# Two of the first-layer weight transfers put on ScalarE's queue, the last weight piece moved forward on SyncE's, and half a dummy matmul ahead of layer 1

## Chip, cores, metric

One core of one Trainium2 chip. The metric is device time in microseconds (us) of one execution. A run counts as slow when it lies over 1.5% above the fastest of the same kernel. Some kernels lose a stretch of full TensorE clock in some runs, and each run's mean granted clock (1.0, or less) tells which. Where a kernel has both kinds of run, its full-clock runs are compared with full-clock runs.

## The reference

```python
B, S, D, F = 1, 2048, 448, 1792            # x, w1 [D,F], b1, w2 [F,D], b2, all bf16
def reference(x, w1, b1, w2, b2):
    h = jnp.einsum("bsd,df->bsf", x, w1) + b1
    h = gelu_tanh(h)
    return jnp.einsum("bsf,fd->bsd", h, w2) + b2
```

## The kernel before

The 2048 rows go through in four chunks of 512. For the first chunk x is loaded plainly and turned by TensorE; the other chunks come by transposing transfers. D = 448 is three blocks of 128 rows of w1 and a remainder of 64. The matmuls use half the array's rows each (64 of 128) and run in pairs. F is 14 tiles of 128 columns. w1's three full blocks arrive in three pieces: tiles 0 to 3 (384 KB), 4 to 7 (384 KB), 8 to 13 (576 KB). The 64 remainder rows arrive in two: tiles 0 to 3 (64 KB) and 4 to 13 (160 KB), and VectorE copies some of each to the other half of the partitions.

```python
        W1CUTS = (0, 4, 8, 14)
        def load_w1(i):
            c0, c1 = W1CUTS[i] * P, W1CUTS[i + 1] * P
            pr.dma("sync", lambda e: e.dma_start(
                w1_sb[:, :, c0:c1], w1[0:D3, c0:c1].rearrange("(k p) f -> p k f", p=P)), ("w1", i))
        RCUTS = (0, 4, 14)
        def load_w1r(i): ...                      # the remainder rows, same form
        # ... (cut)
        pr.dma("sync", lambda e: e.dma_start(xn[:, :, :], x0v), "x")
        load_w1(0)
        load_w1r(0)
        load_w1(1)
        load_w1r(1)
        load_w1(2)
        load_w2(0, 7)
        load_w2(7, 14)
        # ... (cut): b2, then the transposing loads of x
        pr.dma("scalar", ... b1n ..., after=["b1z"])
        pr.op("scalar", lambda e: e.activation(junk[:, :], one, ACT.Gelu_apprx_tanh))   # brings the table load
        # ... (cut)
        warm(NWARM)          # 7 dummy matmuls of 512 columns
        warm(1, HC)          # and one of 256, while x comes
        turn_all()           # 12 + 2 transposes of x, copied out by VectorE and ScalarE
        turn_b1()
        # ... (cut)
        for h in (0, HC):    # layer 1, chunk 0: pairs of F tiles L[0], L[1], ...
            L[0].a(h, h + HC)
            L[1].a(h, h + HC)
        L[0].b()             # ends with the remainder rows
        L[2].a()             # first use of w1's second piece
        L[1].b()
        for j in range(3, NPAIR):
            L[j].a()         # L[4].a: first use of the last piece
            L[j - 1].b()     # L[2].b: first use of the second remainder rows
```

## Time and profile before

| | before |
|---|---|
| time, median of 3 runs | 94.44 us (94.21 to 94.9) |
| span of the profiled run | 93.3 us |
| TensorE busy | 90.0 us, 96% |
| TensorE idle from the first layer-1 matmul to the last | none |
| first piece of w1 issued, landed | 1.18, 6.0 us |
| second piece of w1 issued, landed, used | 2.25, 7.85, 7.99 us |

In the chain of work that ended last each line is a start, a duration and what ran or was waited for. In the timeline the bracket at the end of a line holds how long the engine stood still just before and what released it. SPq and ACTq are the DMA issues of SyncE and ScalarE; a merged line "x2" is two instructions in a row. The two 384 KB pieces of w1 have the same name (w_sb), and are told apart by their issue time.

### The profile page before, as it was taken

Reading aid. Unit: us, or ns where it says so; the run is one execution under the profiler, and the core shown is the slowest. Engines: PE = TensorE matmul, PEld = TensorE weight load, DVE = VectorE, ACT = ScalarE, POOL = GpSimd, SP = SyncE. Lnnn points to the kernel's source line nnn. Section 1 sums busy time; section 2 is a strip of 40 time slices with the busy share of each in tenths; the row PEclk is TensorE's granted clock in tenths of the full one; section 3 lists DMA queues with packets and bytes.
Section 4 is the critical chain, followed back from the end, with each engine's and each line's share of the span. In section 5 each row is a group of like instructions: output and inputs, shape, how many; then the busy total and the mean of one; then the engine's idle time right before and its main releaser. Section 6 shows DMA issues by size and latency. Waiting matters only on the chain.

```text
span 93.3 us, 2058 instructions
## 1 busy us (share of the span) xinstructions
PE 90.0 (96%) x931; PEld 46.6 (50%) x931; DVE 13.4 (14%) x33; ACT 38.5 (41%) x63; POOL 1.1 (1%) x7
## 2 busy tenths in 40 slices
PE   6989999999999999999999999999999999999990
PEld 2475444555554444555554444555554444475890
DVE  0174001100333000000334000000234000000421
ACT  3373787800003787900002887900001878910001
POOL 4000000000000000000000000000000000000000
PEclk9999999999999999999999999999999999999999
DMA  2999999645657000000033000000022000000022
GB/s 48 323 270 303 378 342 137 124 102 113 63 97 212 0 0 0 7 0 0 0 102 101 0 0 4 0 7 0 0 98 98 0 7 0 0 0 7 19 79 98
DMA packets 12340, 7.32 MB, mean 78 GB/s; under 512 B 6956, under 2 KB 12140, under 8 KB 12332
## 3 DMA queue, kind: packets, MB, share of 16 engines
q1 hardware_dynamic: 12304, 7.20, 31.5%
q8 instruction: 7, 0.11, 0.5%
q14 instruction: 1, 0.01, 0.0%
q10 hardware_dynamic: 28, 0.00, 0.0%
HBM read 3.79 MB, written 1.84 MB: 60 GB/s over the span
## 4 chain that ended last, share of the span: by engine, by line
PE 96%; ACT 1%; DVE 0%; issue 0%
PE u L215 91%; PE u L190 4%; PE u L337 1%; ACT xT L344 1%; DVE out_sb L324 0%
## 5 line engine op out<-in xcount | busy, mean ns | idle before, releaser
L267 ACT ACTIVATE g<-u,b_f 128x512 bf16<-128x512 f32 x56 | 35.0, 685 | 40.1 <-PE u L215 40.1
L215 PE MATMUL u<-w_sb,g 64*128 64x448 bf16 (+1 forms) x504 | 43.2, 328 | 0.0
L215 PE MATMUL u<-xT,w_sb 64*128 64x512 bf16 (+1 forms) x348 | 40.9, 369 | 0.3 <-ACT xT L344 0.3
L215 PEld LDWEIGHTS u<-w_sb,g 64*128 64x128 bf16 x504 | 24.5, 94 | 18.4
L215 PEld LDWEIGHTS u<-xT,w_sb 64*128 64x128 bf16 x348 | 16.9, 94 | 19.4 <-DMA w_sb<-in_w_dram 0.6
L310 DVE TENSOR_TENSOR out_sb<-u,b_bc 128x448 bf16<-128x448 f32 x14 | 8.1, 620 | 60.8 <-PE u L215 60.8
L215 PE MATMUL u<-xT,w1r 64*128 64x512 bf16 x56 | 10.6, 376 | 0.0
L215 PEld LDWEIGHTS u<-xT,w1r 64*128 64x128 bf16 x56 | 2.8, 94 | 3.4
L327 ACT CAST out_sb<-u 128x224 bf16<-128x224 f32 x1 | 0.3, 345 | 9.2 <-PE u L215 9.2
L190 PE MATMUL u<-const-bfloat16-1.0 128*128 128x512 bf16 (+1 forms) x8 | 3.4, 599 | 0.8 <-PEq L441 0.8
L190 PEld LDWEIGHTS u<-const-bfloat16-1.0 128*128 128x128 bf16 x8 | 1.0, 136 | 2.4 <-issue 2.4
L175 ACT ACT_TABLE_LOAD x1 | 1.3, 1283 | 1.6 <-DVE b1n L172 1.6
L344 ACT COPY xT<-u 128x384 bf16<-128x384 bf16 x2 | 1.0, 479 | 1.9 <-PE u L337 1.9
L337 PEld LDWEIGHTS u<-ident,xn 128*128 128x128 bf16 x12 | 1.2, 144 | 0.6 <-issue 0.6
L337 PE MATMUL u<-ident,xn 128*128 128x128 bf16 x12 | 1.4, 310 | 0.0
L185 DVE COPY xT<-xT 64x512 bf16<-64x512 bf16 x3 | 0.9, 290 | 3.5 <-DMA xT<-in_x_dram 3.4
L404 DVE COPY b_z<-b_bc 1x448 bf16<-1x448 bf16 x1 | 0.3, 268 | 5.4 <-DMA b_bc<-in_b_dram 5.4
L318 DVE TENSOR_TENSOR out_sb<-u,b_bc 128x448 bf16<-128x448 f32 x1 | 0.6, 624 | 1.7 <-PE u L215 1.7
L179 DVE STREAM_TRANSPOSE b1t<-b1n 32x32 bf16<-32x32 bf16 x4 | 0.8, 202 | 0.1
L344 DVE COPY xT<-u 128x384 bf16<-128x384 bf16 x2 | 0.7, 358 | 0.7 <-PE u L337 0.7
L367 ACT COPY xT<-u 64x256 bf16<-64x256 bf16 x2 | 0.7, 368 | 0.0
L380 DVE COPY w1r<-w1r 64x256 bf16<-64x256 bf16 (+1 forms) x2 | 0.6, 288 | 0.9 <-DMA w1r<-in_w_dram 0.9
(17 smaller groups left out, 4.1 us busy)
## 6 DMA issues: line engine op xcount, KB each, us to landing
out_dram<-out_sb SPq DMA_DIRECT2D x16, 112.0 KB, 1.7
w_sb<-in_w_dram SPq DMA_DIRECT2D x2, 784.0 KB, 8.9
w_sb<-in_w_dram SPq DMA_DIRECT2D x2, 384.0 KB, 5.2
w_sb<-in_w_dram SPq DMA_DIRECT2D x1, 576.0 KB, 6.7
xn<-in_x_dram SPq DMA_DIRECT2D x1, 448.0 KB, 3.2
xT<-in_x_dram SPq DMA_TRANSPOSE x12, 4.2
w1r<-in_w_dram SPq DMA_DIRECT2D x1, 160.0 KB, 5.9
b_bc<-in_b_dram SPq DMA_DIRECT2D x1, 112.0 KB, 8.8
```

The source lines that it names most:

```text
L175: pr.op("scalar", lambda e: e.activation(junk[:, :], one, ACT.Gelu_apprx_tanh))
L179: pr.op("vector", lambda e, q=q: e.transpose(b1t[32 * q:32 * q + 32, :], b1n[:, 32 * q:32 * q + 32]), after=["b1n"], event=("b1t", q))
L185: pr.op("vector", lambda e: e.tensor_copy(xT[0:H, KT, s0:s1], xT[H:P, KT, s0:s1]), after=after, event=event)
L190: pr.op("tensor", lambda e: e.matmul(unit[2][:, 1, 0:cols], lhsT=ones_w, rhs=ones_m[:, 0:cols], start=True, stop=True))
L215: o = pr.op("tensor", lambda e: e.matmul(unit[u][:, lo, cols], lhsT=lhsT, rhs=rhs, start=start, stop=stop, skip_group_check=skip), after=a ...
L267: pr.op("scalar", lambda e, lo=lo, ft=ft: e.activation(g[:, ft, c * SC:(c + 1) * SC], unit[u][:, lo, :], ACT.Gelu_apprx_tanh, bias=b1_f[:, ...
L310: pr.op("vector", lambda e, lo=lo, j=j: e.tensor_tensor(out=out_sb[:, j, :], in0=unit[u][:, lo, 0:D], in1=b2_bc[:, :], op=ALU.add), after= ...
L318: pr.op("vector", lambda e: e.tensor_tensor(out=out_sb[:, j, :].rearrange("p (two h) -> p two h", two=2), in0=unit[u][:, :, 0:DH], in1=b2_ ...
L337: pr.op("tensor", lambda e, k=k: e.transpose(stage(t)[:, k * P:(k + 1) * P], xn[:, t, k * P:(k + 1) * P], ident[:, :]), after=["ident", "x ...
L344: pr.op(engine, lambda e: e.copy(o, i) if engine == "scalar" else e.tensor_copy(o, i), after=[("xt", t)], event=("xT0", t))
L367: e.copy(o, i) if engine == "scalar" else e.tensor_copy(o, i),
L380: pr.op("vector", lambda e, odd=odd: e.tensor_copy(odd(slice(0, H)), odd(slice(H, P))), after=[("w1r", i)], event=("w1rU", i))
```

## The change

The intent: let ScalarE, which has nothing to do early, issue what layer 1 needs second; let SyncE get to the large last piece sooner; keep TensorE busy in the 0.32 us before layer 1. The dummies write to another PSUM buffer because the later one would otherwise hit a buffer that is still being read.

```diff
-        def load_w1(i):
+        def load_w1(i, engine="sync"):
...
-            pr.dma("sync", lambda e: e.dma_start(
+            pr.dma(engine, lambda e: e.dma_start(
...   (load_w1r likewise)
         load_w1(0)
-        load_w1r(0)
-        load_w1(1)
+        load_w1(2)
         load_w1r(1)
-        load_w1(2)
         load_w2(0, 7)
...
         pr.op("scalar", lambda e: e.activation(junk[:, :], one, ACT.Gelu_apprx_tanh))
+        load_w1r(0, "scalar")
+        load_w1(1, "scalar")
...
-                pr.op("tensor", lambda e: e.matmul(unit[2][:, 1, 0:cols], ...
+                pr.op("tensor", lambda e: e.matmul(unit[0][:, 0, 0:cols], ...
...
         turn_all()
+        warm(1, HC)
         turn_b1()
```

More of the change, by code (lines that the diff above doesn't have):

```diff
@@ L126, in w1_of, with load_w1r @@
             return max(i for i, c in enumerate(W1CUTS) if c <= ft)
-        def load_w1(i):
+        def load_w1(i, engine="sync"):
             c0, c1 = W1CUTS[i] * P, W1CUTS[i + 1] * P
-            pr.dma("sync", lambda e: e.dma_start(
+            pr.dma(engine, lambda e: e.dma_start(
                 w1_sb[:, :, c0:c1], w1[0:D3, c0:c1].rearrange("(k p) f -> p k f", p=P)), ("w1", i))
         RCUTS = (0, 4, 14)
-        def load_w1r(i):
+        def load_w1r(i, engine="sync"):
             cs = slice(RCUTS[i] * P, RCUTS[i + 1] * P)
-            pr.dma("sync", lambda e: e.dma_start(w1r[H:P, cs], w1[D3:D, cs]), ("w1r", i))
+            pr.dma(engine, lambda e: e.dma_start(w1r[H:P, cs], w1[D3:D, cs]), ("w1r", i))
         def load_w2(a, b):
@@ L189, in warm @@
             for _ in range(n):
-                pr.op("tensor", lambda e: e.matmul(unit[2][:, 1, 0:cols], lhsT=ones_w, rhs=ones_m[:, 0:cols],
+                pr.op("tensor", lambda e: e.matmul(unit[0][:, 0, 0:cols], lhsT=ones_w, rhs=ones_m[:, 0:cols],
                                                    start=True, stop=True))
```

## The prediction

> **What bounds the kernel now.** I read the page's busy shares and the chain that ended last first, then the first 17 us of the timeline, then the DMA issues with their times to landing. The chain says where the time is:
>
> ```profile
> PE 90.0 (96%) x931; PEld 46.6 (50%) x931; DVE 13.4 (14%) x33; ACT 38.5 (41%) x63; POOL 1.1 (1%) x7
> ...
> 0.73 0.04 issue
> 0.77 3.36 PE u L190 x8
> 4.13 1.37 PE u L337 x12
> 5.50 0.02 issue
> 5.53 0.49 ACT xT L344
> 6.01 0.01 issue
> 6.02 85.08 PE u L215 x909
> 91.10 0.38 DVE out_sb L324
> ```
>
> The reader is to see one long run of TensorE work, 6.02 to 91.10, with nothing between. The change touches none of the layer matmuls, so those 85.1 us stay unless a weight comes late and cuts a hole into them. What can be won is ahead of 6.02: 0.77 us of start, eight dummies, twelve transposes of x, and a gap. The timeline shows the gap and what lies on both sides (columns: start, busy us, engine, line, operation, count, idle before and releaser):
>
> ```profile
> 4.05 1.44 PE L337 MATMUL u<-ident,xn 128*128 128x128 bf16 x12
> ...
> 5.28 0.42 PE L358 MATMUL u<-ident,xr 128*128 128x128 bf16 x2
> ...
> 6.02 1.64 PEld L215 LDWEIGHTS u<-xT,w_sb 64*128 64x128 bf16 x30 [0.58 <-DMA w_sb<-in_w_dram]
> 6.02 2.13 PE L215 MATMUL u<-xT,w_sb 64*128 64x256 bf16 x30 [0.32 <-ACT xT L344]
> ```
>
> TensorE stands from 5.70 to 6.02. The two releasers named differ: the matmul line blames ScalarE's copy (ends 6.01), the weight-load line the DMA of w1. In the code the first half of layer 1 needs only x tiles 0 and 1, whose copies end at 4.93 and 5.36; so the true gate is w1's first piece. The DMA issues agree: it is issued at 1.18 and has the shortest landing of the group, 4.8 us, so it lands at 1.18 + 4.8 = 6.0.
>
> The next gates, from issue start plus time to landing, against first use in the timeline:
> - First remainder rows: 1.65 + 4.7 = 6.35; used by a VectorE copy at 7.68, which VectorE reaches only after b1's transposes. Slack 1.3 us.
> - Second piece of w1: 2.25 + 5.6 = 7.85 (5.6 because the two 384 KB transfers have 5.2 in the middle and one is 4.8); its weight load is at 7.99. Slack 0.15 us. This is the tight one.
> - Second remainder rows: 2.87 + 5.9 = 8.8; used at about 10.8, with a 0.35 us copy between. Slack 1.6 us.
> - Last piece: 3.41 + 6.7 = 10.1; used at about 11.0 (six groups of matmuls further on). Slack 0.9 us.
>
> ```profile
> 2.25 0.58 SPq L130 DMA_DIRECT2D w_sb<-in_w_dram  x1
> ...
> 7.99 1.18 PEld L215 LDWEIGHTS u<-xT,w_sb 64*128 64x128 bf16 x12
> ...
> 8.80 0.35 DVE L380 COPY w1r<-w1r 64x640 bf16<-64x640 bf16 x1 [0.89 <-DMA w1r<-in_w_dram]
> ```
>
> **What the Trainium skill says.** (1) "DMA: Bandwidth & Descriptors", section Issuing engines are not separate DMA queues: transfers of either queue run on the same 16 engines and interleave; a second queue saves only issue time. The trace agrees in so far as the engines are full: DMA share 0.9 to 1.1 from 2.5 to 4.5 us. (2) Same page, section Queues, rings and completion order: an engine takes turns between queues that have work. The only ScalarE transfer before, b1, is issued at 0.95 and its 28 packets move at 3.1 to 3.6 us, side by side with w1's first 1 KB packets; this fits taking turns, and also plain order of arrival, so the trace does not decide it. (3) "Advanced Engine Details and Errata", section Sequencer Loop: an engine instruction is pushed into a queue and the sequencer goes on to read the next. If that holds for the table load, "behind the table load" is only program order and the ScalarE issues come at about 1.7 us, not 2.9. No run here shows it yet. (4) "TensorE: Matmul & The Clock Gate", section Part 1: the array starts at half clock and is released after a busy window of about 3.4 us whose phase is free. The trace agrees: the 128-column transposes come every 0.107 us (1.2 GHz) up to 5.44, and the 256-column matmuls from 6.02 last 269 ns, against 418 ns for the half dummy of the same 256 columns while cold.
>
> **The change part by part.**
> - Dummy target moved to another PSUM buffer: no instruction more or less; 0 us. It has to move because the new dummy would otherwise write where x tile 3 is still being copied out.
> - Half a dummy ahead of layer 1: 256 columns cold. Cold full dummies of 512 columns come every 0.42 us in the timeline, so half is 0.21 us. It fits after the last transpose's issue slot (about 5.55 to 5.76), inside the 5.70 to 6.02 gap: 0 us on the path if w1 lands at 6.0, and it fixes the earliest start of layer 1 at about 5.76. So the most that an earlier w1 can bring is 6.02 - 5.76 = 0.26 us. It also keeps the array busy, for the clock.
> - SyncE loses two issues ahead of the last piece, 0.55 + 0.58 plus gaps = 1.2 us; the last piece goes out at about 1.65 instead of 3.41, the second remainder rows at about 2.3 instead of 2.87. Neither w1's first piece nor x moves: they are still first and second.
> - ScalarE gains two issues of about 0.55 us. Its next work is the copy of x tile 1 at 4.88, so they are hidden if they start at 1.7 (done 2.9) or at 3.1 (done 4.3).
> - Bytes are the same. x and the first piece are 832 KiB = 852 kB; the DMA bytes of the half-microsecond windows reach 852 kB at 4.6 us, and the landing of the first piece is 1.35 us after that. In the windows from 4.6 to 5.0, while the first remainder rows move (64 packets), the rate is only some 150 GB/s, later 318 while the second piece moves, about 290 for the last piece. Two queues could fill the weak stretch.
>
> Now the second piece, if ScalarE issues at 3.1 and 3.7: first data about 1 us after an issue starts (x: issued 0.73, moving by 1.8), so the remainder rows from about 4.2, then the second piece, beside the last piece on SyncE. 65 + 393 = 458 kB at half of an estimated 350 GB/s is 2.6 us: done 6.8, landing 1.3 to 1.5 later, 8.1 to 8.3. Needed 7.99, or 7.73 if layer 1 starts 0.26 sooner. That is a hole of 0.1 to 0.5 us, which eats the gain. If ScalarE gets more than half, or two queues reach 380 GB/s (the rate of the w2 stretch), it is about none.
>
> Sum for this middle course: -0.26 to 0 at the start, 0 to +0.4 at the second piece, 0 elsewhere: about 0 us.
>
> **The rivals.**
> - *A: ScalarE issues early and takes turns with the first piece of w1.* Then from 3.15 on the first piece gets half the rate: 2 x 393 kB at 320 GB/s is 2.5 us, done 5.6 instead of 4.6, landing 6.9 instead of 6.0. Layer 1 starts 0.9 us later, and a gap of over a microsecond may cost the warm clock for a while. Time 95.3, up to 96. For it: point (3) above. Against it: whoever put just half a dummy (0.21 us) there expected a gap of that size, not of one microsecond.
> - *B: the first piece lands sooner and nothing is late.* Its completion came 1.35 us after its bytes, while x's came about 0.8 after its own; the slow remainder rows directly behind it may hold it. With them gone layer 1 starts at 5.76: 94.44 - 0.26 = 94.2, and 94.0 if the fuller array settles the clock sooner in some runs (the spread before, 94.21 to 94.9, may be the phase of that window).
> - *C: hidden anyway.* ScalarE issues at about 3.1, the first piece is undisturbed at 6.0, the second just in time: 94.4.
> - *D: the second piece is late alone*: the hole worked out above, 94.6 to 95.0.
>
> **Range and chances.** I give A 0.25, B 0.3, C 0.25, D 0.2. The middle of these lies near 94.4; the mean is higher, for A is one-sided. The 8 in 10 range takes B's lower end with run-to-run spread (93.8) and A's ordinary case (95.5). 2% is 1.9 us: no gain can reach it, since all idle time of TensorE ahead of layer 1 is some 0.3 us beside dummies that wait for x; a loss could only through A with a clock that falls back. So faster 0.01, within 0.95, slower 0.04.
>
> **What would show each step.** The timeline after: two ScalarE DMA issues either near 1.7 (inside the table load) or near 3.0. The first layer-1 matmul: 5.76 (B), 6.0 (C, D), 6.9 (A). An idle entry "DMA w_sb" on the weight-load row near 8 is D; none is B or C. The matmul total of layer work stays 85.1 us plus such holes. The second remainder rows and the last piece must land before 10.4 and 11.0; if TensorE stops there, the slacks above were wrong. The prediction is wrong if the clock turns out cold after 6.02 (256-column matmuls near 418 ns), if x itself lands later than 3.94 because ScalarE's transfers share with it, or if ScalarE's copies of x start late behind its DMA issues.

## The result, and the profile after

| | before | after |
|---|---|---|
| median of 4 runs | 94.67 us (94.21 to 95.25) | 99.25 us (98.2 to 99.66) |
| ratio of fast runs, 95% interval | | 1.0463 (1.0359 to 1.0568) |
| span of the profiled run | 93.3 us | 98.1 us |
| granted clock by run | 1.0 (profiled run) | 0.982, 0.983, 0.983, 1.0 |

A ratio is the mean time of one kernel's fast runs over that of the other's of the same rounds, so it is not quite the ratio of the medians. The change made the kernel 4.6% slower; the prediction had 94.4 with 93.8 to 95.5, and a chance of 4% for slower by more than 2%.

The chain of waits of the changed kernel, its last four steps:

```profile
2.23 9.07 DMA w_sb<-in_w_dram
11.30 0.05 issue
11.35 84.59 PE u L215 x877
95.94 0.38 DVE out_sb L324
```

A transfer of w1, 9.07 us long, has taken the place of the dummies, transposes and early layer-1 matmuls. It was issued at 2.23, so it is the second piece. The timeline shows who issued what when, and what TensorE did:

```profile
1.19 0.95 SPq L130 DMA_DIRECT2D w_sb<-in_w_dram  x2
1.60 1.28 ACT L173 ACT_TABLE_LOAD   x1 [1.60 <-DVE b1n L170]
1.68 0.52 ACTq L137 DMA_DIRECT2D w1r<-in_w_dram  x1
...
2.23 0.60 ACTq L130 DMA_DIRECT2D w_sb<-in_w_dram  x1
...
5.83 2.13 PE L215 MATMUL u<-xT,w_sb 64*128 64x256 bf16 x30
...
8.68 0.64 PE L215 MATMUL u<-xT,w1r 64*128 64x512 bf16 x2 [0.71 <-DMA w1r<-in_w_dram]
...
11.35 1.58 PE L215 MATMUL u<-xT,w_sb 64*128 64x512 bf16 x12 [2.03 <-DMA w_sb<-in_w_dram]
```

Three things are to be seen. ScalarE's two issues are not behind the table load: they start at 1.68 and 2.23 while it runs from 1.60 to 2.88, nearly the times (1.65, 2.25) at which SyncE issued the same transfers before. Layer 1 starts at 5.83, 0.19 us sooner than before. And then TensorE stands twice, 0.71 us for the first remainder rows and 2.03 us for the second piece. The DMA issues give the landings (last number: us from issue to landing):

```profile
w_sb<-in_w_dram SPq DMA_DIRECT2D x1, 576.0 KB, 8.4
...
w_sb<-in_w_dram SPq DMA_DIRECT2D x1, 384.0 KB, 4.3
w_sb<-in_w_dram ACTq DMA_DIRECT2D x1, 384.0 KB, 9.1
...
w1r<-in_w_dram ACTq DMA_DIRECT2D x1, 64.0 KB, 7.0
```

The first remainder rows land at 1.68 + 7.0 = 8.7 (6.35 before), the second piece at 2.23 + 9.1 = 11.3 (7.85 before), the last piece at about 1.65 + 8.4 = 10.05 (10.1 before). The last piece was issued 1.8 us sooner and landed no sooner; its early issue bought only the right to go first.

The loss does not stop there. Busy time by stage of the changed kernel (columns: stretch and length, PE, PEld, DVE, ACT, POOL busy with counts, then granted clock, DMA share, GB/s):

```profile
9.30:11.35 2.05, 0.02 (x2) 0.01 (x2) 0.35 (x1) 1.07 (x2) 0.00 (x0) 1.00 1.10 322
11.35:12.50 1.15, 1.15 (x12) 0.56 (x14) 0.00 (x0) 0.00 (x0) 0.00 (x0) 1.00 1.09 379
12.50:15.90 3.40, 3.40 (x20) 1.27 (x18) 0.27 (x1) 1.27 (x2) 0.00 (x0) 0.51 1.40 240
...
21.46:95.94 74.48, 74.43 (x801) 38.75 (x797) 9.30 (x18) 28.03 (x46) 0.00 (x0) 1.00 0.12 32
```

From 12.5 us on, 1.15 us after TensorE went on, it runs at half clock for 3.4 us: fully busy, it does half the work that this time would have held. From layer 2 of the first chunk on the kernels are alike: 21.46 to 95.94 here and 16.62 to 91.10 before are both 74.48 us.

**The account of the 4.8 us of span.** The first matmul that uses the second piece starts at 11.35 instead of 8.21: 3.14 us. From there to the last matmul it takes 84.59 us instead of 82.89: 1.70 us, half of the 3.4 at half clock. Sum 4.84. The 0.71 us hole and the 0.19 us won at the start are inside the 3.14, for whatever happens before the second piece lands is overtaken by that wait.

### The profile page after: what moved, and what is told of

The parts are those of the page before. It is cut to its first block, busy times and chain, and to the rows that moved or that the text cites. A ratio compares the mean times of both kernels' runs of the same rounds, so it can differ in the third digit from the quotient of the medians.

```text
span 98.1 us, 2060 instructions
## 1 busy us (share of the span) xinstructions
PE 92.4 (94%) x932; PEld 47.2 (48%) x932; DVE 13.4 (14%) x33; ACT 38.6 (39%) x63; POOL 1.1 (1%) x7
## 4 chain that ended last, share of the span: by engine, by line
PE 86%; DMA 9%; ACTq 1%; ACT 1%; DVE 1%; issue 0%
PE u L215 86%; DMA w_sb<-in_w_dram 9%; ACTq L171 1%; ACT L173 1%; DVE out_sb L324 0%; DVE b1n L170 0%
## 5 line engine op out<-in xcount | busy, mean ns | idle before, releaser
L215 PE MATMUL u<-xT,w_sb 64*128 64x512 bf16 (+1 forms) x348 | 42.3, 378 | 2.0 <-DMA w_sb<-in_w_dram 2.0
L215 PE MATMUL u<-xT,w1r 64*128 64x512 bf16 x56 | 11.3, 391 | 0.7 <-DMA w1r<-in_w_dram 0.7
L173 ACT ACT_TABLE_LOAD x1 | 1.3, 1283 | 1.6 <-DVE b1n L170 1.6
```

The source lines that it names most:

```text
L215: o = pr.op("tensor", lambda e: e.matmul(unit[u][:, lo, cols], lhsT=lhsT, rhs=rhs, start=start, stop=stop, skip_group_check=skip), after=a ...
```

## The experiments

Theory O (order): the second piece is late because the last piece and the second remainder rows were issued ahead of it or with it; transfers move about in the order of issue, whichever queue. Theory Q (queue): what ScalarE issues is served worse beside SyncE's. Theory T (turns): both queues take turns from when both have work.

### e1_order: everything on SyncE, in the changed order

```diff
         load_w1(0)
         load_w1(2)
+        load_w1r(0)
         load_w1r(1)
+        load_w1(1)
...
-        load_w1r(0, "scalar")
-        load_w1(1, "scalar")
```

> All loads on SyncE's queue, in about the order in which the changed kernel issued them (x, first piece, last piece, first remainder rows, second remainder rows, second piece). Theory O (order: the engines serve transfers about in the order of issue, whichever queue): the second piece still lands only after some 2016 KiB, at 10 to 11.3 us, TensorE stands some 2 to 3 us before it, time 97.5 to 99.5. Theory Q (queue: what ScalarE issues is served worse beside SyncE's): with one queue the late landing shrinks to what the bytes ahead cost, no stretched landing of the first remainder rows, time 96 to 97.

Measured 98.44 us median (97.42 to 99.66), ratio 1.0335 (1.03 to 1.037). The runs fall into two kinds: 97.42 and 97.84 at clock 1.0, and 99.66 and 99.04 at clock 0.983. The second kind was slow and is not in the ratio; it fits the half-clock stretch, as in three of the changed kernel's four runs (3.4 us at half clock in some 98 us make a mean of 0.983). Compared kind with kind: 99.0 to 99.7 in both kernels with it; 97.4 and 97.8 here against 98.2 there without. The chain of e1_order, profiled in a full-clock run:

```profile
3.40 7.57 DMA w_sb<-in_w_dram
10.97 0.05 issue
11.02 82.91 PE u L215 x877
```

The second piece lands at 10.97, and the 877 matmuls after it take 82.91 us where the changed kernel needed 84.59. ScalarE's queue is not needed for the loss: the order alone brings most of it. (On one queue, a later place is also a later issue: 3.40 instead of 2.25.) The first remainder rows are late as well (copied at 9.34), so theory Q's account of that fails too.

### e2_queue: both queues as changed, the order put right

```diff
...   (load_w1 and load_w1r take `after` and pass it on)
-        load_w1(2)
+        load_w1(2, after=["junk"])      # SyncE waits for ScalarE's first activation, at about 3.1 us
...
         pr.op("scalar", lambda e: e.activation(junk[:, :], one, ACT.Gelu_apprx_tanh), event="junk")
```

> The changed kernel, but SyncE holds the last piece back until ScalarE's first activation is over (about 3.1 us), so that the remainder rows and the second piece on ScalarE's queue are issued ahead of it (1.7 and 2.2). Same queues, other order. Theory O: second piece lands at 7.9 or before, no hole, layer 1 at 5.8 to 6.0, time 94.2 to 94.8. Theory Q: once the last piece's transfers come (from about 4.2) ScalarE's ring starves again, second piece lands at 9.5 or later, time 96 to 99.

Measured 94.39 us median of 12 runs, ratio 1.0001 (0.9978 to 1.0024): the whole loss is gone with the same transfers on the same queues. ScalarE's second piece, issued at 2.27, lands 5.2 us later, at 7.5. Packets of the two queues (q1 SyncE, q10 ScalarE) between 4.5 and 6.5 us, first in the changed kernel, then in e2_queue (columns: packets, MB, share of the time of the 16 DMA engines):

```profile
q1 hardware_dynamic: 320, 0.45, 73.8%
q10 hardware_dynamic: 52, 0.05, 7.8%
```

```profile
q10 hardware_dynamic: 424, 0.41, 65.3%
q1 hardware_dynamic: 129, 0.18, 29.0%
```

This is the picture of the cause. Both queues had work issued in both kernels; in this stretch the one whose transfer was issued first moved most of the packets. It holds in both directions, so a lower rank of ScalarE's queue does not explain the loss. It is not a strict order, though: in the changed kernel the queues moved 376 (SyncE) and 339 (ScalarE) packets from 6.5 to 9.0 us, side by side. Packets can also be told apart by size in the packed trace (rows of w2 are 896 B): when the last packet of the second piece was through, at 10.72, some 561 kB of w2, issued after it, had moved too. In e2_queue it was none.

### e3_dummy: the dummy part alone, on the kernel before

```diff
         turn_all()
+        warm(1, HC)
...     (dummies to unit[0], as in the change)
```

> The kernel before with the half dummy and the moved dummy target alone. Both theories: it sits in the 0.32 us gap, layer 1 at 6.0, time within 0.3 us of before, 94.2 to 95.0.

Measured 94.71 us median of 12 runs, ratio 1.0016 (0.9994 to 1.0038): no difference that 12 runs would show, and so no part of the 4.6%. In its profile layer 1 started at 5.51, not 6.0, because the first piece landed at 5.5 in that run and the dummies were through by then: its half dummy took 0.27 us against 0.40 in the changed kernel, for the full clock came sooner. The landing wanders: 6.0 in before, 5.5 in the changed kernel, 5.1 in e1_order, 6.2 in e2_queue, always with only x ahead of it on its queue.

### e4_late: ScalarE's issues really behind the table load

```diff
...   (`after` and the event "junk" as in e2_queue)
-        load_w1r(0, "scalar")
-        load_w1(1, "scalar")
+        load_w1r(0, "scalar", ["junk"])
+        load_w1(1, "scalar", ["junk"])
```

> The changed kernel, but ScalarE's two issues wait for the first activation, so that they are really behind the table load, at about 3.1 and 3.7 us, when SyncE has already issued half of w2. Theory O: the second piece now also stands behind w2's first half (784 KB, some 2.1 us at 378 GB/s): lands at 13 to 13.5, time 100.5 to 102. Theory T (the two queues take turns packet by packet as soon as both have work, so the issue time hardly matters since ScalarE's packets only moved from 4.7 us on): lands at about 11.3 as in the changed kernel, time 98 to 99.7.

Measured 101.62 us median (101.24 to 101.94), ratio 1.0756 (1.0716 to 1.0795): the time that theory O gave. All four runs lost full clock (0.966 in three, 0.983 in one; in the profile from 11.1 to 17.9 us), which is part of the loss. The issues are at 3.15 and 3.76:

```profile
2.77 1.34 SPq L140 DMA_DIRECT2D w_sb<-in_w_dram  x2
3.15 0.58 ACTq L137 DMA_DIRECT2D w1r<-in_w_dram  x1
3.76 0.82 ACTq L130 DMA_DIRECT2D w_sb<-in_w_dram  x1
...
11.22 0.86 PE L215 MATMUL u<-xT,w1r 64*128 64x512 bf16 x2 [3.14 <-DMA w1r<-in_w_dram]
...
13.22 2.74 PE L215 MATMUL u<-xT,w_sb 64*128 64x512 bf16 x12 [1.14 <-DMA w_sb<-in_w_dram]
```

Issued 1.5 us later, the second piece lands 1.9 us later, at 13.2, although in the changed kernel ScalarE's packets hardly moved before 6.5. Theory T, which had it land at 11.3 again, falls: none of ScalarE's packets moved from 4.5 to 6.5 us, though both its transfers had been issued. But theory O in its strict form falls too, and its number was partly luck. It counted only w2's first half ahead of the second piece; both halves were issued before 3.76. And both landed after it (issue durations in ns, first and last issue in us; then us from issue to landing):

```profile
L140 SPq DMA_DIRECT2D w_sb<-in_w_dram x2: 578/650/723, 2.8 to 3.4; - x2
DMA to landing us min/median/max: 10.6/11.3/11.9
```

The first half, issued at 2.8, landed at 13.4 or later, the second, issued at 3.4, at 14.0 or later; the second piece had landed at 13.2. From 9 to 11 us (`prof e4_late --dma --window 9:11`) the two queues moved nearly alike:

```profile
q1 hardware_dynamic: 376, 0.34, 60.4%
q10 hardware_dynamic: 290, 0.29, 49.7%
```

So in these runs what was issued earlier had a head start, and then the queues ran side by side. Putting ScalarE's issues really behind the table load made things worse.

### e5_fill: dummies in the second hole

```diff
         L[0].b()
+        for _ in range(9):
+            pr.op("tensor", lambda e: e.matmul(unit[3][:, 1, 0:SC], lhsT=ones_w, rhs=ones_m[:, 0:SC],
+                                               start=True, stop=True))
         L[2].a()
```

> The changed kernel with nine full dummies (some 1.9 us at full clock) on TensorE in its second hole, where it stood 2.03 us for the second piece of w1. The transfers are untouched. If the half-clock stretch (12.5 to 15.9 us, 1.7 us lost) comes from TensorE standing idle through most of one window of the clock gate, it goes: clock 1.0 in every run, time 97.3 to 98.3. If it has another cause, some runs keep it and the median stays near 99.2.

Measured 98.21 us median (97.86 to 98.43), ratio 1.0375 (1.0336 to 1.0414), clock 1.0 in all four runs. The changed kernel's three half-clock runs average 99.38 (99.45, 99.66, 99.04), its one full-clock run is 98.2. So the half-clock stretch is worth about 1.2 us of median time and comes from TensorE standing idle, for the edit leaves the issues of the transfers as they were and fills only the hole (four runs of each kernel). It is a repair of the symptom: the wait itself stays.

```profile
9.71 2.07 PE u L389 x9
11.78 82.84 PE u L215 x877
```

### e6_fourth: the last piece fourth on SyncE again

```diff
-        load_w1(2)
         load_w1r(1)
+        load_w1(2)
```

> The changed kernel with the last piece of w1 fourth on SyncE again, behind the second remainder rows. The last piece is then issued at about 2.2, just when ScalarE issues the second piece (2.23), not 0.6 us before it. Theory O: the two share the stretch, second piece lands between 8.0 and 10 us, first remainder rows at 7.0 or sooner, time 94.6 to 96.5. Theory Q: no gain by this, second piece still near 11, time 98 to 99.5.

Measured 97.43 us median (96.98 to 98.67; one of four runs at clock 0.982, not in the ratio), ratio 1.028 (1.0235 to 1.0325). A miss for both theories: the time is between their ranges, the second piece landed at 2.25 + 8.83 = 11.08, where theory Q had it, and the first remainder rows at 1.67 + 6.4 = 8.1, later than the 7.0 of theory O. The chain:

```profile
2.25 8.83 DMA w_sb<-in_w_dram
```

Here SyncE issued the last piece and ScalarE the second piece at the same moment, 2.25. They landed at 9.95 and 11.08, 1.1 us apart, hardly closer than in the changed kernel (10.05 and 11.3), where the last piece had been issued 0.6 us ahead. From 6.5 to 9 us the queues moved 369 (SyncE) and 314 (ScalarE) packets: they shared, and my range for theory O had left out that two which share both end late. Whether SyncE's queue is favoured at equal issue stays open. Moving the last piece back by one place is not enough; in e2_queue, 0.9 us behind the second piece was enough. In this profile the first piece landed late as well (7.0; TensorE stood 1.58 us), which no theory here explains.

### e7_third: a third of the last piece third

```diff
-        W1CUTS = (0, 4, 8, 14)
+        W1CUTS = (0, 4, 8, 10, 14)
...
         load_w1(2)
         load_w1r(1)
+        load_w1(3)
```

> Dose: the changed kernel, but only a third of the last piece (192 of 576 KB) goes third on SyncE, the rest behind the second remainder rows. Then 1632 KiB go out up to the end of the second piece, against 1280 (landing 7.85, before) and 2016 (landing 11.33, changed). Theory O, by a straight line between these: second piece lands at 9.5, first remainder rows at 7.1, one hole of about 1.5 us, no half-clock stretch, time 95.5 to 96.5. Theory Q: second piece at 11, time 98 or more.

Measured 97.01 us median (96.69 to 99.02; one of four runs at clock 0.983, not in the ratio), ratio 1.0241 (1.0197 to 1.0284), which leaves the 2% verdict unclear. The time missed theory O's range, and the half-clock run was not expected either. The second piece landed at 2.23 + 8.0 = 10.2: between the 7.85 and 11.33 of the two ends, as theory O has it and Q does not, but 0.7 later than the straight line. TensorE stood 0.4 us for the remainder rows (landed 1.68 + 6.3 = 8.0, line: 7.1) and 1.6 us for the piece. That line ends in the changed kernel's own late landing. A line through the two landings of the kernel before (7.85 for 1280 KiB, 10.1 for 2016) gives 8.9. So the bytes ahead explain the direction and about 1.1 of the 2.4 us of delay; the rest is not settled.

### e8_split: a try to beat both

```diff
-        W1CUTS = (0, 4, 8, 14)
+        W1CUTS = (0, 2, 4, 8, 14)
```

with all loads on SyncE in the order of need.

> A try to beat both: the kernel before with the first piece of w1 cut into two of 192 KB, all on SyncE in the order of need. By theory O the first half lands some 0.5 us sooner, layer 1 starts at 5.6 instead of 6.0 and its later pieces arrive as before: 94.0 to 94.4, ratio 0.995 to 1.0. If the gate is not the first piece, or the extra issue delays the second piece: 94.5 to 95.

Measured 94.75 us median of 22 runs, ratio 1.0022 (1.0002 to 1.0042): not faster, a miss. Layer 1 did start sooner, at 5.66, but the extra issue pushed the second piece from 2.25 to 2.77, it landed at 8.75 instead of 7.85, with the same bytes ahead of it, and TensorE then stood 0.4 us for it. The later issue is 0.5 of these 0.9 us; the smaller packets of the halved piece (512 B for 1 KB) are a rival for the rest that no run tested. What was won at the first gate was paid at the second, whose slack had been 0.15 us. No version tried beats the kernel before.

## Why the prediction was wrong

**What held.** The bound, the gates and their slacks before the change were read rightly: the second piece, with 0.15 us, was named as the tight one, and it broke; the first remainder rows, with 1.3 us, broke too (landing 8.7 for 6.35, TensorE stood 0.71 us). Half a dummy is free (e3_dummy). Layer 1 started at 5.83, near the 5.76 named as its earliest; that limit is one of a cold clock, for with the clock released sooner it started at 5.51 in e3_dummy and 5.54 in e7_third. The work from layer 2 on did not change (74.48 us). The ScalarE issues came early, inside the table load, as point (3) of the prediction allowed; the consequence drawn from it in rival A, that the first piece of w1 would lose half its rate and land at 6.9, did not come: it landed at 5.5. It had been issued first.

**The step that failed** is the one in the change part by part: "65 + 393 = 458 kB at half of an estimated 350 GB/s is 2.6 us: done 6.8, landing 1.3 to 1.5 later, 8.1 to 8.3." It gave ScalarE's transfers half of the engines from about 4.2 us, for issues at 3.1 and 3.7. e4_late is that case: none of their packets moved from 4.5 to 6.5 us, and the second piece landed at 13.2. The changed kernel issued at 1.68 and 2.23, for which the prediction had worked out only the first piece (rival A) and not the second. There ScalarE's queue moved 52 of 372 packets between 4.5 and 6.5 us: the last piece had been issued at 1.65, before them, and went first. The hole of "0.1 to 0.5 us" became a start 3.14 us later. The mechanism named for rival D, a late second piece, was right; its size was off by a factor of more than six, and its chance was put at 0.2. A smaller term of the same sum was misread: "landing 1.3 to 1.5 later" comes from the 1.35 us between 852 kB and the first piece's landing, but those bytes are of all transfers together. By its own packets (1 KB on SyncE's queue of the changed kernel) the first piece was through at 5.14 and landed at 5.5; the second was through at 10.72 and landed at 11.3. So 0.4 to 0.6 us, and rival B's late completion was not there to be won.

The figure for the right estimate stood in the profile before. The last piece landed there at 10.1, when 448 + 384 + 64 + 384 + 160 + 576 = 2016 KiB had gone out. In the changed order the second piece ends the same 2016 KiB, so 10.1 was to be expected for it, some 2.3 us later than its 7.85 for 1280 KiB. The measured 11.0 (e1_order) to 11.3 is a further 0.9 to 1.2 us, not explained.

**The second failed step** is "a loss could only through A with a clock that falls back". A did not happen, and the wait for the second piece passed 2% without any fall of the clock: the full-clock run took 98.2 us, 3.7% over 94.67. The clock fell back besides, in three of four runs, after waits of 0.71 and 2.03 us in the profile; that cost 1.7 us there and about 1.2 us of the median (e5_fill).

**What stays open.** Why the second piece lands another 0.9 to 1.2 us beyond what the bytes ahead of it explain. Part of it may be w2, which moved beside it: 561 kB by 10.72 in the changed kernel, against 214 kB by the time the last piece was through (9.59) in the kernel before; but in e1_order it was only 292 kB, and the landing was 0.9 us late as well. How far issue order and turns mix is not known. The packed trace has packets by queue and size, not by engine, so whether a few of the 16 engines lag cannot be read. Nor was it shown why the first piece's landing wanders between 5.1 and 7.0 us.

## What to carry to other kernels

Count the bytes that are issued ahead of a transfer over all queues together, in order of issue time, and read from the old profile when that many bytes had landed: here that came nearer (10.1, measured 11.0 to 11.3) than a share of the bandwidth (8.1 to 8.3). It is a first estimate: the landing came 0.9 to 1.3 us later than it in the changed kernel, e1_order, e7_third and e8_split, and 0.4 us sooner in e2_queue; in e4_late the order did not hold. The second queue gave no second lane here: a large transfer that is needed late should be issued after a small one that is needed soon, and in another queue it must be made to wait for that (e2_queue). And a stall of 2 us can cost more than itself: here its half-clock aftermath was another 1.2 us of the median.

## What the Trainium skill lacked or had wrong

- "DMA: Bandwidth & Descriptors", section Queues, rings and completion order, says that an engine takes turns between queues that have work. What it lacks is from when on an issued transfer counts as work. In these runs what had been issued first mostly moved first, from 4.5 to 6.5 us: 320 packets against 52 in favour of SyncE's queue in the changed kernel, 424 against 129 in favour of ScalarE's in e2_queue. Later the queues did run side by side (376 and 339 from 6.5 to 9 us in the changed kernel, 376 and 290 from 9 to 11 us in e4_late). The trace does not show the engines one by one, so turns on each engine are neither confirmed nor refuted.
- "ScalarE: Activation LUTs", section What ACT_TABLE_LOAD costs, gives 1283 ns, which the profile has to the digit, but does not say whether a DMA issue behind the load on ScalarE's queue waits for it; the page of the prediction's point (3) has it only for instructions in general. It did not wait: issues at 1.68 and 2.23 inside a load from 1.60 to 2.88.
- "TensorE: Matmul & The Clock Gate", section HAM oscillation, warns of idle gaps over about 3.4 us. Shorter gaps were enough here: with 0.71 and 2.03 us in the changed kernel's profile half clock followed, in three of its four runs, and it went when the longer one was filled (e5_fill). In e1_order, whose full-clock profile has two gaps of 1.0 us, two of four runs lost clock; these were not profiled.
